# Interleaving the first two query chunks of a gated attention mix, with three more unused products at the start and 500 exponential tiles on VectorE

## The chip, the cores and the metric

The kernel runs on one core of one Trainium2 chip. The metric is the device time of one execution in microseconds (us). Engines are named as the profile names them: PE (TensorE, matrix products), ACT (ScalarE), DVE (VectorE), POOL (GpSimd), SP (SyncE, which here only issues transfers).

## The reference

The input x has 2048 tokens of 512 values, in bfloat16. Two branches share it, with 32 heads of 16 values each, and a gate mixes them:

```python
g = sigmoid((x * gate_w).sum(-1))
# branch A: softmax attention
q, k, v = split(x @ A_wqkv)
a = merge(softmax(q @ k.T * 16**-0.5) @ v) @ A_wo
# branch B: linear attention with learned features
pq, pk = q_B @ w_phi, k_B @ w_phi
phi = concat(softmax(p), softmax(-p))          # for pq and pk
b = merge((phi_q @ (phi_k.T @ v_B)) / (phi_q @ phi_k.sum(s) + 1e-6)) @ B_wo
out = g * a + (1 - g) * b
```

Branch A needs 32 x 2048 x 2048 exponentials; they are most of the work.

## The kernel before

**Tiles and passes.** The queries are cut into 4 chunks of 512 (`qc`), the keys into 16 tiles of 128 (`kt`). The 32 heads stand as 4 groups of 8 (`cp`, 128 rows of the projected q and k), and each group has two sides, so that 4 heads of one side lie in the four 32-row strips of PE. One pass `g` of 32 is a chunk, a group and a side; it has 16 rows `p` (one for each key tile) of 4 units (one for each head). A unit is a score tile of 128 keys x 512 queries. There are 512 rows and 2048 units. Before, the passes run through all four groups of chunk 0, then chunk 1, and so on.

**Two ways to an exponential.** Most units go to ACT: a PE product into one of four PSUM banks that form a ring (`_qk`, L1015), an exponential over two units at a time, 128x1024 (`_exp`, L1063), and one product with the values (`_pv`, L1122). `NUMS` gives for each pass how many of its 64 units go to DVE instead. These are taken in batches of four (`_vector_batch`): a score product into one of the other four PSUM banks, one DVE instruction that turns scores into bits of an exponential (128x512, L922), two DVE steps on the whole batch (128x2048 and 128x4096, L947), and four products with the values for each unit instead of one.

**Projections.** For each group, the keys of all 2048 tokens are projected before its first pass: 4 blocks, each with 4 products of 512 columns and one DVE copy out of PSUM (`_proj_k`, L698 and L770). Values are projected for two groups together: 8 blocks, each with 8 products of 256 columns, one DVE copy, and one POOL instruction for a scaled second copy (`_proj_v`, L809, L819, L826). Queries are projected for one chunk and group at a time (`_proj_q`): 4 products, one DVE copy (L783) and two POOL maskings (L788). `due` and `urgent` are counted in rows `p`: with one group after the other, group `cp` is first used in row 32 x `cp`.

**The rest.** The gate is computed once (`_gate`; its last part is four small DVE copies, L862). Branch B projects keys and queries in eight pairs of token tiles each, with a chain on DVE, POOL and ACT (L1281 to L1357), and its numerators are mixed into the outputs (`_out`, L1599). When a pass ends, DVE transposes its sums out of PSUM (L1143); every two passes are normalised on DVE and POOL (L1151 to L1160), and SP issues 16 small transfers and one transposing transfer into `onTA`.

**The order.** `Plan.order` places every operation in Python before the kernel runs: each engine gets a fixed queue, from the operations' modelled costs, `prio` (due row), `rel` and `urgent`. A pseudo-random shift of the due rows comes from `SEEDS`. Operations named in `PORT` on DVE are not placed beside a POOL operation. At run time each engine works through its queue in order and waits on semaphores. `filler` and `pad` put products with zeros (L1129), or unused products (L1035), into PE's queue where it would be little used; `PADK` is the number of the first ACT product that may be padded. `_warm` issues nine unused products at the start while the first part of x is loaded.

Of the kernel before, what the change touches and what calls it, by code (L numbers as in the profile page):

```python
# [10 lines left out]
P = 128  # L11
# [54 lines left out]
class Plan:  # L66
# [70 lines left out]
        self.ops.append(o)  # L137
        return o

    SEEDS = (6713, 8236, 795, 8928, 4203, 3987, 4548, 4431, 3369, 6855, 1992, 9096, 3816, 673, 8476, 4153, 2488, 5053, 9892, 380, 9864, 6961, 8928, 7398, 8610, 6258, 6732, 8778, 7190, 2318, 6568, 0, 527, 0)  # L140

    def shift(self):
        count = {}
# [30 lines left out]
    SAME = 100  # L174
    OPEN = 2
    HURRY, FREE = 20, 30
    PORT = ("v_step", "b_neg", "b_max", "b_sub", "b_sum", "b_total", "b_mul", "n_mul", "n_den", "kvbd")
    HOLDING = ("kproj", "qproj", "bv", "pq", "vproj", "outa", "outb", "wtr", "xtr")

    def rank(self, o):  # L180
# [227 lines left out]
class _Kernel:  # L408
# [13 lines left out]
    P_BACK, RATIO, BV = 1, 1, 8  # L422
    DEN, KV2, P_MAX = 1, 0, 0
    REND = 5
    P_M, P_BMUL, CHUNKS = 0, 0, 2
    GDUE = 26
    VMIN = 8
    FAST = 3
    VSOON = -2
    PADK = 8  # L430
    LAST, FIRST_OUT, NEXT_OUT, DEP_OUT = 0, 8, 0, 2
    ALONE, EARLY = 12, 10
    PVP = 10
# [1 line left out]
    def __init__(self, nc, A_x, A_wqkv, A_wo, B_wqkv, B_w_phi, B_wo, gate_w, out):  # L435
        self.nc = nc
        self.x2d = A_x.flatten_outer_dims()
        self.A_wqkv, self.A_wo = A_wqkv, A_wo
        self.B_wqkv, self.B_w_phi, self.B_wo = B_wqkv, B_w_phi, B_wo
        self.gate_w, self.out2d = gate_w, out.flatten_outer_dims()  # L440
        self.S = self.x2d.shape[0]
        self.NT = self.S // TOK
        self.NQC = self.S // QCH
        self.NPACK = self.NQC * 8 * self.NT
        self.plan = Plan()

    def build(self):
        with ExitStack() as ctx:
# [233 lines left out]
        job.bank = bank  # L682
        return job, (job if bank is None else None)

    def _warm(self, n, after):

        def run(e):
            for _ in range(n):
                ins = e.matmul(self.ps[:, 4, :], self.warm[:, 0:P], self.warm[:], start=True, stop=True)  # L689
            return ins  # L690
        self.plan.op("PE", run, 0.427 * n, reads=[self.b_warm], deps=[after], name="warm", prio=-99)

    COLS = 0

# [44 lines left out]
    def _proj_q0(self, half, bank):  # L739

        lo, op, ends = 256 * half, self.plan.op, []
        job, pool = self._job(bank)
        m = None
        for c in range(4):
            m = op("PE", lambda e, c=c: e.matmul(self._bank(job)[:, 0:256], self.WA[:, 0, c, 0:P],
                                                 self.xT[:, c, lo:lo + 256], start=(c == 0), stop=(c == 3)),
                   self.c_pe(256), reads=[self.b_x0[half], self.b_WA[0][0]], deps=[m], name="qproj", prio=half - 2.2,
                   acquire=None if c else pool)
            m.urgent = half - 99
        for side in range(2):  # L750
            dst, by = self.qT[:, side, lo:lo + 256], self.mask[:, side:side + 1]
            if half or side:
                o = op("DVE", lambda e, dst=dst, by=by: e.tensor_scalar(dst, self._bank(job)[:, 0:256], by, None,
                                                                        op0=ALU.mult), self.c_dve(256) + 0.06,
                       deps=[m] + ends, reads=[self.b_mask], name="q0_ev", prio=side - 2, release=pool if side else None)
            else:
                o = op("ACT", lambda e, dst=dst, by=by: e.activation(dst, self._bank(job)[:, 0:256], ACT.Copy, scale=by),
                       self.c_act(256) + 0.1, deps=[m], reads=[self.b_mask], name="q0_ev", prio=-2)
            self.b_qT[side].writers.append(o)
            if side == 0:  # L760
                self.b_q0[half].writers.append(o)
            ends.append(o)
        self.early.setdefault(bank, []).extend(ends)

    def _proj_k(self, cp, j):
        due = 32 * cp + 3 * j - self.KDUE if cp else 4 * j - 2.0
        self._proj(lambda c: self.WA[:, 1, c, P * cp:P * cp + P],
                   lambda c: self.xT[:, c, QCH * j:QCH * j + QCH],
                   [self.b_xT[j], self.b_WA[1][cp > 0]],
                   [lambda e, b: e.tensor_copy(self.kT[:, cp, QCH * j:QCH * j + QCH], b)],  # L770
                   self.c_dve(512), due, due - (24 if cp else 99), "kproj", [self.b_kT[cp][j]],
                   urgent=32 * cp + 4 * j - self.SOON)

    def _proj_q(self, qc, cp):
        n = qc * 4 + cp
        due = 32 * n - self.QDUE
        s0 = 2 * (n % (self.NQS // 2))

        lhs, rhs = lambda c: self.WA[:, 0, c, P * cp:P * cp + P], lambda c: self.xT[:, c, QCH * qc:QCH * qc + QCH]
        reads = [self.b_xT[qc], self.b_WA[0][cp > 0], self.b_mask]  # L780
        if self.P_Q:
            tmp, b_tmp = self.qtmp[:, n % 2, :], self.b_qtmp[n % 2]
            o = self._proj(lhs, rhs, reads, [lambda e, b: e.tensor_copy(tmp, b)], self.c_dve(512), due, 32 * n - 30, "qproj",  # L783
                           [b_tmp], urgent=32 * n - self.SOON)
            o.deps += [r for r in b_tmp.readers if r not in o.deps]
            b_tmp.readers = []
            for side in range(2):
                x = self.plan.op("POOL", lambda e, side=side: e.tensor_scalar(  # L788
                    self.qT[:, s0 + side, :], tmp, self.mask[:, side:side + 1], 0.0, op0=ALU.mult, op1=ALU.add), 0.7,
                    reads=[b_tmp, self.b_mask], writes=[self.b_qT[s0 + side]], name="qmask", prio=due + 1)  # L790
                x.urgent = o.urgent
            return
        self._proj(lhs, rhs, reads,
                   [lambda e, b: e.tensor_tensor(self.qT[:, s0:s0 + 2, :], b[:, None, :].to_broadcast([P, 2, QCH]),
                                                 self.mask[:, :, None].to_broadcast([P, 2, QCH]), ALU.mult)],
                   self.c_dve(1024), due, 32 * n - 30, "qproj", [self.b_qT[s0]], urgent=32 * n - self.SOON)
        self.b_qT[s0 + 1] = self.b_qT[s0]

    def _proj_v(self, pr, t0):

        op, NT = self.plan.op, self.NT
        job = Job()
        due = 64 * pr + t0 - (self.VDUE if pr else 0.5)
        mm = None
        for tt in range(2):
            def run(e, tt=tt):
                out = self._bank(job).rearrange("p (c t x) -> p c t x", c=2, t=2)[:, :, tt, :]
                for c in range(4):
# [2 lines left out]
                return ins  # L811
            mm = op("PE", run, 4 * self.c_pe(256), reads=[self.b_xT[t0 // 4], self.b_WA[2][pr]], deps=[mm], name="vproj",
                    prio=due, rel=due - 24 if pr else 0 if t0 < 4 else -99, acquire=None if tt else job)
            mm.urgent = 64 * pr + t0 - self.VSOON
        lo, n = t0 * self.VCP, 2 * self.VCP
        both = lambda v: v[:, 2 * pr * NT * self.VCP:(2 * pr + 2) * NT * self.VCP].rearrange(
            "p (c x) -> p c x", c=2)[:, :, lo:lo + n]
# [47 lines left out]
                prio=100))  # L865
        self.b_gB.writers = done

    NUMS = (6, 10, 12, 14, 14, 15, 13, 16, 13, 20, 17, 13, 16, 13, 19, 21, 10, 18, 12, 16, 19, 13, 17, 16, 15, 20, 12, 19, 17, 16, 23, 13)

    def _plan_vector(self):  # L870

# [9 lines left out]
            self.hooks.setdefault(max(0, int(due) - 4), []).append(  # L881
                lambda k=k, units=units, due=due: self._vector_batch(k, units, due))
        for n in range(1, 4 * self.NQC):
            self.hooks.setdefault(max(0, 32 * n - 30), []).insert(0, lambda n=n: self._proj_q(*divmod(n, 4)))
        self.away = set(away)

    def _value_bufs(self, bufs, p, spill):

        kt, cp = p % self.NT, p // (2 * self.NT) % 4
        at = cp * self.NT + kt  # L890
        found = list(bufs[cp][kt // 2].writers)
        if spill and at + 1 < 4 * self.NT:
            found += bufs[(at + 1) // self.NT][(at + 1) % self.NT // 2].writers
        return found

    def _vector_batch(self, number, units, due):
# [46 lines left out]
        for k in range(4):  # L943
# [9 lines left out]
            for g in sorted({u // (4 * NT) for u in units}):  # L953
# [3 lines left out]

                def run(e, g=g, src=src, ot=ot, v=v, tile=tile, place=place):
                    for j, u in src:
                        ins = self._values(e, ot, g % 8, u // 4 % NT, {u % 4: tile[:, place(j), :].bitcast(BF16)}, v)  # L960
                    return ins
                x = op("PE", run, 0.23, reads=[buf], deps=list(found.values()), name="pvx", prio=units[0] / 4 - 2,
                       kind="col", array=0.0533 * len(src), strips=[u % 4 for _, u in src])
# [5 lines left out]
    def _attention(self):  # L969
# [24 lines left out]
        while a < len(self.mine):  # L994
# [4 lines left out]
            done = self.mine[a] if a < len(self.mine) else NU  # L999
            while len(self.pvs) < done // 4:  # L1000
                self._pv(len(self.pvs))
                if len(self.pvs) % (8 * NT) == 0:
                    self._out(len(self.pvs) // (8 * NT) - 1)

    def _unit(self, u):

        p, i = divmod(u, 4)
        g, kt = divmod(p, self.NT)
        qc, g8 = divmod(g, 8)
        s = 2 * ((qc * 4 + g8 // 2) % (self.NQS // 2)) + g8 % 2  # L1010
        return p, i, kt, g8 // 2, s

    def _scores(self, e, u, out, cols=slice(0, QCH)):
# [56 lines left out]
    def _pv(self, p):  # L1070
# [13 lines left out]
        def run(e):  # L1084
            for _ in range(o.filled):
                self._fill(e, ot)
            return self._values(e, ot, g % 8, kt, src, self.V)
        o = self.plan.op("PE", run, 0.23, reads=[self.b_zero], deps=deps, name=f"pv{p}", prio=p + self.PVP, kind="col",
                         acquire=None if kt else ot, array=0.0533 * len(src), strips=list(src))
        plan = self.plan  # L1090
# [40 lines left out]
        return ins  # L1131

    def _norm_a(self, g, last):
        qc, g8 = divmod(g, 8)
        return self._norm(qc, lambda: self._bank(self.ot[g]), g8 % 2, last, self.onTA[:, qc % 3, g8 // 2, :],
                          self.b_onTA[qc % 3][g8 // 2], 16 * g + 17.0, self.ot[g], g >= self.NPACK // self.NT - 2)

# [430 lines left out]
    def _out(self, qc):  # L1568
        op, NT, NQC = self.plan.op, self.NT, self.NQC
        for tt in range(4):  # L1570
            t = 4 * qc + tt
            final = qc == NQC - 1
            due = max(128 * (qc + 1) + 8 + 4 * tt, self._num_due(t) + 8)
            job, first = self.outs[t]
            b_onTA = self.b_onTA[qc % 3]
            if final:
# [70 lines left out]
```

## Time and profile before

| | value |
|---|---|
| time, median of 3 runs | 767.77 us (766.18 to 769.58) |
| profiled execution: its time | 767.62 us |
| profiled execution: span, first to last instruction | 765.6 us |
| ACT busy | 749.1 us, 804 instructions |
| DVE busy | 711.6 us, 1110 instructions |
| PE busy | 739.6 us, 7149 products |
| POOL busy | 207.5 us |
| mean granted PE clock | 0.997 |
| ACT exponentials (L1063) | 782 instructions, 720.4 us |
| DVE tiles (L922) and their steps (L947) | 488 and 244 instructions, 313.7 and 235.4 us |
| first exponential starts, last one starts | 8.22 us, 756.5 us |

Busy time is the union of an engine's or a group's instruction spans. Consecutive instructions of an engine overlap by some tens of ns, so a mean duration times a count is more than the busy time. A PE product's span holds the time to pass through the array, and products overlap; PE's busy share says little of how full it is.

### The profile page before, as it was taken

The numbers are of one execution on the slowest core, as the hardware profiler recorded it, in microseconds if no ns is written. First come the engines' busy times: TensorE is split into PE (matmuls) and PEld (weight loads), VectorE is DVE, ScalarE is ACT, GpSimd is POOL, SyncE is SP. The second block draws the span as 40 slices with busy tenths as digits, with TensorE's granted clock in tenths as the row PEclk, the third lists the DMA queues.
The fourth block names the chain that finished last, engine by engine and source line by source line (L and its number), as shares of the span: only waits on it lengthen the run. The fifth ranks groups of instructions, "written<-read, shape, count | busy, mean of one in ns | idle before, by whom it ended". The sixth has DMA issues, their size and how long they took to land.

```text
span 765.6 us, 17042 instructions
## 1 busy us (share of the span) xinstructions
PE 739.6 (97%) x7149; PEld 219.6 (29%) x7220; DVE 711.6 (93%) x1110; ACT 749.1 (98%) x804; POOL 207.5 (27%) x301
## 2 busy tenths in 40 slices
PE   8999999999999999999999999999999999999998
PEld 3322233222222222222332322232222222222222
DVE  4778997899999999999999999999999999999995
ACT  6999999999999999999999999999999999999996
POOL 2210255315053260405145023422314140250000
PEclk9999999999999999999999999999999999999999
DMA  9501001000000000010121202211111121011000
GB/s 232 127 2 28 3 14 15 1 2 8 9 3 14 1 3 14 1 15 2 15 29 28 53 11 51 45 27 30 32 26 28 29 47 24 15 30 27 5 12 28
DMA packets 89180, 20.78 MB, mean 27 GB/s; under 512 B 83472, under 2 KB 88592, under 8 KB 89104
## 3 DMA queue, kind: packets, MB, share of 16 engines
q1 hardware_dynamic: 87232, 18.92, 13.4%
q8 instruction: 56, 0.92, 0.5%
q10 hardware_dynamic: 1872, 0.79, 0.4%
q14 instruction: 20, 0.16, 0.1%
HBM read 4.21 MB, written 2.10 MB: 8 GB/s over the span
## 4 chain that ended last, share of the span: by engine, by line
ACT 76%; PE 15%; DVE 9%; issue 1%
ACT ET L1063 73%; PE ps L1015 5%; PE ps L1122 5%; PE ps L698 3%; ACT bq L1310 3%; DVE vs L922 3%; DVE vs L947 2%; PE ps L1129 1%; PE ps L689 1%; DVE onB L1475 1%; DVE T L1143 0%; DVE bq L1307 0%; DVE btree L1304 0%; DVE ghB L862 0%; DVE qtmp L783 0%
## 5 line engine op out<-in xcount | busy, mean ns | idle before, releaser
L1063 ACT ACTIVATE ET<-ps 128x1024 bf16<-128x1024 f32 (+1 forms) x782 | 720.4, 1154 | 3.7 <-PE ps L1015 3.6
L922 DVE TENSOR_SCALAR vs<-ps 128x512 uint16<-128x512 f32 x488 | 313.7, 679 | 20.7 <-PE ps L1015 19.7
L1015 PE MATMUL ps<-qT,kT 32*128 32x512 bf16 (+1 forms) x2052 | 312.4, 385 | 13.1 <-ACT ET L1063 8.0
L947 DVE TENSOR_SCALAR vs<-vs 128x2048 uint16<-128x2048 uint16 (+1 forms) x244 | 235.4, 977 | 1.9 <-PE ps L1122 0.5
L1122 PE MATMUL ps<-vs,V 128*32 128x512 bf16 x1952 | 216.4, 384 | 1.4 <-DVE vs L947 1.4
L1122 PE MATMUL ps<-ET,V 128*32 128x512 bf16 x1560 | 194.5, 387 | 0.1
L1015 PEld LDWEIGHTS ps<-qT,kT 32*128 32x128 bf16 x2052 | 78.0, 91 | 309.3 <-ACT ET L1063 293.2
L1314 POOL TENSOR_TENSOR btree<-btree 128x512 f16<-128x512 f16 (+1 forms) x32 | 33.4, 1044 | 188.8 <-DVE btree L1312 188.0
L1122 PEld LDWEIGHTS ps<-ET,V 128*32 128x32 bf16 x1560 | 48.9, 94 | 84.1 <-issue 75.8
L1129 PE MATMUL ps<-kT,zero 128*32 128x512 bf16 x628 | 63.4, 385 | 0.0
L1122 PEld LDWEIGHTS ps<-vs,V 128*32 128x32 bf16 x1952 | 49.8, 95 | 45.9 <-issue 27.5
L1299 POOL TENSOR_SCALAR bq<-bq 128x1024 bf16<-128x1024 bf16 x16 | 21.5, 1341 | 150.6 <-DVE bq L1281 119.5
L698 PE MATMUL ps<-WB,xT 128*128 128x512 bf16 x160 | 49.6, 383 | 2.8 <-issue 2.1
L1160 POOL TENSOR_TENSOR T<-T,rinv 128x512 bf16<-128x512 f32 x15 | 18.2, 1210 | 83.4 <-DVE rinv L1158 83.2
L698 PE MATMUL ps<-xT,WA 128*128 128x512 bf16 x101 | 33.2, 392 | 1.9 <-issue 1.6
L788 POOL TENSOR_SCALAR qT<-qtmp,mask 128x512 bf16<-128x512 bf16 x30 | 25.8, 866 | 28.8 <-DVE qtmp L783 28.5
L1143 DVE STREAM_TRANSPOSE T<-ps 128x512 f32<-128x512 f32 x32 | 22.6, 707 | 11.2 <-PE ps L1122 11.1
L1310 ACT ACTIVATE bq<-bq 128x2048 bf16<-128x2048 bf16 x16 | 32.1, 2007 | 0.2
L1281 DVE CAST bq<-ps 128x512 bf16<-128x512 f32 x32 | 21.7, 680 | 0.3 <-PE ps L698 0.2
L826 POOL TENSOR_SCALAR V<-V 128x544 bf16<-128x544 bf16 x16 | 12.6, 788 | 33.4 <-DVE V L819 33.2
L698 PEld LDWEIGHTS ps<-WB,xT 128*128 128x128 bf16 x192 | 13.3, 97 | 25.3 <-issue 20.5
L1129 PEld LDWEIGHTS ps<-kT,zero 128*32 128x32 bf16 x628 | 14.7, 94 | 19.7 <-issue 18.8
(88 smaller groups left out, 405.3 us busy)
## 6 DMA issues: line engine op xcount, KB each, us to landing
T<-T SPq DMA_DIRECT2D x240, 8.0 KB, 1.8
WB<-in_B_wqkv_dram SPq DMA_DIRECT2D x1, 1536.0 KB, 7.9
out_dram<-WB SPq DMA_DIRECT2D x12, 128.0 KB, 1.7
WA<-in_A_wqkv_dram SPq DMA_DIRECT2D x2, 384.0 KB, 5.4
WoB<-in_B_wo_dram SPq DMA_DIRECT2D x1, 512.0 KB, 3.8
WoA<-in_A_wo_dram SPq DMA_DIRECT2D x1, 512.0 KB, 4.8
WA<-in_A_wqkv_dram ACTq DMA_DIRECT2D x2, 128.0 KB, 3.1
WA<-in_A_wqkv_dram ACTq DMA_DIRECT2D x1, 256.0 KB, 4.6
```

What stands on the lines that cost most here:

```text
L698: return e.matmul(out, lhs, rhs, start=start, stop=stop)
L788: x = self.plan.op("POOL", lambda e, side=side: e.tensor_scalar(self.qT[:, s0 + side, :], tmp, self.mask[:, side:side + 1], 0.0, op0=ALU.m ...
L922: bits = lambda e, to, src: e.tensor_scalar(to, src, SCALE * LOG2E * 128.0, float(ORIGIN), op0=ALU.mult, op1=ALU.add)
L947: o = op("DVE", lambda e, k=k, src=src, dst=dst: e.tensor_scalar(dst, src, float(STEPS[k - 1]), None, op0=ALU.add), 0.16 + k * n * QCH * 0 ...
L1015: return e.matmul(out[:, cols], self.kT[32 * i:32 * i + 32, cp, kt * TOK:(kt + 1) * TOK], self.qT[32 * i:32 * i + 32, s, cols], start=True ...
L1063: o = plan.op("ACT", lambda e: e.activation(self.ET[:, a % NS:a % NS + n, cols], self.ps[:, a % NR:a % NR + n, cols], ACT.Exp, scale=SCALE ...
L1122: ins = e.matmul(self._bank(ot)[32 * i:32 * i + 32, :], v[:, v0:v0 + 32], tile, start=(kt == 0), stop=(kt == self.NT - 1), tile_position=( ...
L1129: ins = e.matmul(self._bank(ot)[32 * i:32 * i + 32, :], self.zero[:], self.kT[:, 0, 0:QCH], start=False, stop=False, tile_position=(0, 32 ...
L1143: t1 = op("DVE", lambda e: e.transpose(T1[:, side].rearrange("p b s -> p (b s)"), src()), 0.735, deps=last, writes=[b_T1[side]], name="n_t ...
L1281: [lambda e, b, k=k: e.tensor_copy(bq[:, k].rearrange("p (g s v) -> p g s v", g=8, s=2)[:, :, 0, :], b.rearrange("p (g v) -> p g v", g=8))],
L1310: op("ACT", lambda e: e.activation(flat, flat, ACT.Exp), 1.789, reads=[b], writes=[b], name="b_exp", prio=due + 1)
L1314: + [("b_sum", two(128 * n), lambda e, n=n: e.tensor_tensor(half[:, :, 0:n], half[:, :, 0:n], half[:, :, n:2 * n], ALU.add), (n <= self.P_ ...
```

## The change

Chunks 0 and 1 are interleaved: the passes now go through group 0 of chunk 0, group 0 of chunk 1, group 1 of chunk 0, group 1 of chunk 1, and so on; chunks 2 and 3 stay as they were. Group `cp` is then first used in row 64 x `cp`, and the due rows of its key and value projections follow. The first value block of the second half keeps an earlier due row, because a read of 32 columns runs on into it. `_warm` is used a second time: three unused products behind the first half of the first query projection. `PADK` goes from 8 to 2, the gate's copies and `gwb` join `PORT`, `NUMS` gives 500 units to DVE instead of 488 (+11 in passes 0 to 7, -5 in 8 to 15, +6 in 16 to 23, none in 24 to 31), and `SEEDS` is another list.

```diff
-    PORT = (..., "n_mul", "n_den", "kvbd")
+    PORT = (..., "n_mul", "n_den", "kvbd", "gate_b", "gwb")
...
+    PAIRQ = 1
...
-    PADK = 8
+    PADK = 2
...
+        pairs = [(qc, cp) for cp in range(4) for qc in range(2)] if self.PAIRQ else [(qc, cp) for qc in range(2) for cp in range(4)]
+        self.pairs = pairs + [(qc, cp) for qc in range(2, self.NQC) for cp in range(4)]
+        self.seq = [(qc, 2 * cp + side) for qc, cp in self.pairs for side in range(2)]
+        self.use = [32 * next(n for n, x in enumerate(self.pairs) if x[1] == cp) for cp in range(4)]
+        self.done = [32 * max(n + 1 for n, x in enumerate(self.pairs) if x[0] == qc) for qc in range(self.NQC)]
...
+        if self.WARM and not half:
+            self.early.setdefault(1, []).append(self._warm(self.WARM, m, bank=1, cost=0.215, prio=-2.15))
...
-        due = 32 * cp + 3 * j - self.KDUE if cp else 4 * j - 2.0
+        due = self.use[cp] + 3 * j - self.KDUE if cp else 4 * j - 2.0
...
-                   urgent=32 * cp + 4 * j - self.SOON)
+                   urgent=self.use[cp] + 4 * j - self.SOON)
...
-        due = 64 * pr + t0 - (self.VDUE if pr else 0.5)
+        use = self.use[2 * pr] + t0
+        if pr and not t0:
+            use = min(use, self.use[1] + 31)
+        due = use - (self.VDUE if pr else 0.5)
...
-    NUMS = (6, 10, 12, 14, 14, 15, 13, 16, 13, 20, 17, 13, 16, 13, 19, 21, 10, 18, 12, 16, 19, 13, 17, 16, 15, 20, 12, 19, 17, 16, 23, 13)
+    NUMS = (6, 10, 16, 14, 14, 16, 16, 19, 13, 19, 17, 12, 17, 11, 19, 19, 14, 20, 12, 16, 19, 13, 17, 16, 15, 20, 12, 20, 17, 16, 22, 13)
...
-                if len(self.pvs) % (8 * NT) == 0:
-                    self._out(len(self.pvs) // (8 * NT) - 1)
+                if len(self.pvs) in self.done:
+                    self._out(self.done.index(len(self.pvs)))
...
-            due = max(128 * (qc + 1) + 8 + 4 * tt, self._num_due(t) + 8)
+            due = max(self.done[qc] + 8 + 4 * tt, self._num_due(t) + 8)
```

More of the change, by code (lines that the diff above doesn't have):

```diff
@@ L138, in op @@
         return o
-    SEEDS = (6713, 8236, 795, 8928, 4203, 3987, 4548, 4431, 3369, 6855, 1992, 9096, 3816, 673, 8476, 4153, 2488, 5053, 9892, 380, 9864, 6961, 8928, 7398, 8610, 6258, 6732, 8778, 7190, 2318, 6568, 0, 527, 0)
+    SEEDS = (3340, 2114, 9789, 849, 7476, 9797, 2928, 4117, 3297, 4434, 5571, 2308, 3491, 3547, 0, 2037, 1043, 5479, 6702, 2263, 0, 95, 4494, 8165, 7230, 4451, 7158, 3400, 9901, 9455, 1584, 0, 4360, 0)
     def shift(self):
@@ L176 @@
     HURRY, FREE = 20, 30
-    PORT = ("v_step", "b_neg", "b_max", "b_sub", "b_sum", "b_total", "b_mul", "n_mul", "n_den", "kvbd")
+    PORT = ("v_step", "b_neg", "b_max", "b_sub", "b_sum", "b_total", "b_mul", "n_mul", "n_den", "kvbd", "gate_b", "gwb")
     HOLDING = ("kproj", "qproj", "bv", "pq", "vproj", "outa", "outb", "wtr", "xtr")
@@ L683, in _job, with _warm @@
         return job, (job if bank is None else None)
-    def _warm(self, n, after):
+    def _warm(self, n, after, bank=4, cost=0.427, prio=-99):
         def run(e):
             for _ in range(n):
-                ins = e.matmul(self.ps[:, 4, :], self.warm[:, 0:P], self.warm[:], start=True, stop=True)
+                ins = e.matmul(self.ps[:, bank, :], self.warm[:, 0:P], self.warm[:], start=True, stop=True)
             return ins
-        self.plan.op("PE", run, 0.427 * n, reads=[self.b_warm], deps=[after], name="warm", prio=-99)
+        return self.plan.op("PE", run, cost * n, reads=[self.b_warm], deps=[after], name="warm", prio=prio)
+    WARM = 3
     COLS = 0
@@ L771, in _proj_k, with _proj_q @@
                    self.c_dve(512), due, due - (24 if cp else 99), "kproj", [self.b_kT[cp][j]],
-                   urgent=32 * cp + 4 * j - self.SOON)
-    def _proj_q(self, qc, cp):
-        n = qc * 4 + cp
+                   urgent=self.use[cp] + 4 * j - self.SOON)
+    def _proj_q(self, n):
+        qc, cp = self.pairs[n]
         due = 32 * n - self.QDUE
@@ L813, in _proj_v @@
                     prio=due, rel=due - 24 if pr else 0 if t0 < 4 else -99, acquire=None if tt else job)
-            mm.urgent = 64 * pr + t0 - self.VSOON
+            mm.urgent = use - self.VSOON
         lo, n = t0 * self.VCP, 2 * self.VCP
@@ L883, in _plan_vector @@
         for n in range(1, 4 * self.NQC):
-            self.hooks.setdefault(max(0, 32 * n - 30), []).insert(0, lambda n=n: self._proj_q(*divmod(n, 4)))
+            self.hooks.setdefault(max(0, 32 * n - 30), []).insert(0, lambda n=n: self._proj_q(n))
         self.away = set(away)
     def _value_bufs(self, bufs, p, spill):
-        kt, cp = p % self.NT, p // (2 * self.NT) % 4
+        kt, cp = p % self.NT, self.pairs[p // (2 * self.NT)][1]
         at = cp * self.NT + kt
@@ L959, in run @@
                     for j, u in src:
-                        ins = self._values(e, ot, g % 8, u // 4 % NT, {u % 4: tile[:, place(j), :].bitcast(BF16)}, v)
+                        ins = self._values(e, ot, self.seq[g][1], u // 4 % NT, {u % 4: tile[:, place(j), :].bitcast(BF16)}, v)
                     return ins
@@ L1008, in _unit @@
         g, kt = divmod(p, self.NT)
-        qc, g8 = divmod(g, 8)
-        s = 2 * ((qc * 4 + g8 // 2) % (self.NQS // 2)) + g8 % 2
+        g8 = self.seq[g][1]
+        s = 2 * (g // 2 % (self.NQS // 2)) + g8 % 2
         return p, i, kt, g8 // 2, s
@@ L1086, in run @@
                 self._fill(e, ot)
-            return self._values(e, ot, g % 8, kt, src, self.V)
+            return self._values(e, ot, self.seq[g][1], kt, src, self.V)
         o = self.plan.op("PE", run, 0.23, reads=[self.b_zero], deps=deps, name=f"pv{p}", prio=p + self.PVP, kind="col",
@@ L1133, in _norm_a @@
     def _norm_a(self, g, last):
-        qc, g8 = divmod(g, 8)
+        qc, g8 = self.seq[g]
         return self._norm(qc, lambda: self._bank(self.ot[g]), g8 % 2, last, self.onTA[:, qc % 3, g8 // 2, :],
```

## The prediction

> **What bounds the kernel now.** I read the page's first two parts, the chain, ACT's and DVE's idle time, then windows. The page, engines and 40 slices:
>
> ```profile
> PE 739.6 (97%) x7149; PEld 219.6 (29%) x7220; DVE 711.6 (93%) x1110; ACT 749.1 (98%) x804; POOL 207.5 (27%) x301
> PE   8999999999999999999999999999999999999998
> ...
> DVE  4778997899999999999999999999999999999995
> ACT  6999999999999999999999999999999999999996
> ```
>
> ACT is full from the second slice to the last but one; DVE has gaps in the first eight slices only. PE's 9 says little, since product spans overlap. The chain that ended last, in order of time:
>
> ```profile
> 14.54 72.58 ACT ET L1063 x79
> ...
> 393.13 2.50 DVE vs L922 x4
> 395.63 0.60 DVE vs L947
> ...
> 396.82 1.14 DVE vs L947
> ```
>
> The chain is ACT's exponentials (73% of the span), one each 72.58/79 = 0.92 us; between 393 and 509 us it runs through DVE and PE. So DVE is nearly co-bound there, at 0.60 to 0.63 us a tile and 0.60 + 1.14 us a batch for the steps. The waits of ACT, and windows by stage:
>
> ```profile
> ACT ET L1063 <- PE ps L1015: 3.6, 6, 1.4
> ```
>
> ```profile
> 0.00:24.00 24.00, 21.75 (x120) 8.20 (x121) 13.12 (x24) 16.64 (x21) 6.26 (x18) 0.93 1.08 235
> 24.00:168.00 144.00, 140.25 (x1214) 43.81 (x1227) 122.35 (x187) 142.61 (x155) 37.04 (x51) 1.00 0.08 17
> 168.00:744.00 576.00, 559.63 (x5672) 162.01 (x5721) 563.08 (x880) 575.05 (x614) 164.17 (x232) 1.00 0.12 21
> 744.00:765.60 21.60, 17.98 (x151) 5.59 (x151) 13.09 (x23) 14.80 (x17) 0.00 (x0) 0.98 0.08 25
> ```
>
> Columns after the length: PE, PEld, DVE, ACT, POOL busy, then PE's clock. ACT loses 3.6 us inside its exponentials in all. DVE's idle time is 10.9, 21.7, 12.9 and 8.5 us: 54.0 together. The first part (x lands) and the last (last values, norm, output) are the same in both programs; the 34.6 us between are what the change can spend.
>
> **ACT's gain.** 12 units leave ACT: 6 exponentials of two units, 782 to 776. At 0.92 us: 5.5 us, all on ACT's path.
>
> **DVE's cost.** 12 tiles at 313.7/488 = 0.643 us, and three batches' steps at 235.4/122 = 1.93 us: 7.7 + 5.8 = 13.5 us. The rows' busy times sum to 765 us where DVE was busy 711.6, as spans overlap, so this is 13.5 x 0.93 = 12.6 us: DVE 724.2 us. With first and last part as before, and 2.0 us from span to time, time = 724.2 + 10.9 + 8.5 + 2.0 + M = 745.6 + M, where M is DVE's idle time in the middle. (Before: 711.6 + 21.4 + 34.6 = 767.6.) For ACT's gain to arrive M must fall to about 16.
>
> **What the interleaving moves.** In the built order, set beside ACT's exponentials, the key blocks of group 1 go from 40-59 us to 83-109, those of group 2 from 86-105 to 142-177, those of group 3 from 148-171 to 233-286, and the second half's values from 99-136 to 130-225. Some ten blocks leave the first 192 us: about 10 x 0.64 us of DVE copies (6.5 us, filled by the 11 new tiles of passes 0 to 7), 4 x 4 products of 0.22 us and six times 8 of 0.11 us on PE (some 8.5 us). That matters since PE is what kept DVE waiting there: the zero products (L1129), which fill PE's spare time, are 8 in the first 168 us, and 620 later. The moved value blocks take their POOL copies (0.79 us each) along; POOL is at 27%. They issue no transfers. In SP's queue the 16 mixing transfers and one transpose per two passes keep their number; near row 225 two transposes of branch B go ahead of one of these. Chunk 0's outputs stay bound by branch B's numerators (row 233). All this at nothing: PE's and POOL's later slack hides it; without that cover the PE part costs its 8.5 us.
>
> **Is there room?** I counted, for each DVE tile, the DVE work queued ahead of it, and ACT's work ahead of its score product in PE's order, with the durations above. The difference is DVE idle time that the order leaves at least. Before: 32.7 us at pass 6 (measured by 168 us: 32.5) and 43.5 at the end, which with the 2.1 us that ACT lost in the middle is the 45.5 measured by 744 us. After: 20.8 at pass 5, then flat, even 20.1 at passes 21 and 22, and 23.0 at the end. So the order asks DVE to run 550 us with no gap at all, beside an ACT with none. Neither can make good what the other loses.
>
> **New stalls.** Before, the same count is flat (37.0 to 37.5) from pass 17 to 25, some 190 us, and ACT lost 0.55 + 0.17 us there. Flat over 550 us: 0.72 x 550/190 = 2.1 us; and 0.7 us where the count falls: 2.8. Lower bound 0 (it can hide nowhere else, but need not occur); upper bound 18, if M stays at 34.6. I take 2.8, by the nearest stretch. The old 0.72 is taken out against it.
>
> **The gate's copies.** ACT's longest stall, 1.39 us, is here (timeline):
>
> ```profile
> 89.92 2.01 DVE L862 COPY ghB<-gh 32x16 f32<-32x16 f32 x4
> 89.97 1.06 POOL L1160 TENSOR_TENSOR T<-T,rinv 128x512 bf16<-128x512 f32 x1 [0.62 <-DVE rinv L1158]
> ...
> 92.70 0.38 PE L1015 MATMUL ps<-qT,kT 32*128 32x512 bf16 x1 [1.28 <-DVE kT L770]
> ...
> 94.20 2.94 ACT L1063 ACTIVATE ET<-ps 128x1024 bf16<-128x1024 f32 x3 [1.39 <-PE ps L1015]
> ```
>
> Four copies in a row, two slowed beside POOL, hold up a key copy, PE's queue behind it, and ACT. Afterwards the copies stand apart between tiles, and keys are due twice as late. Between 0 and 1.4 us; I take 1.4.
>
> **The start.** The windows there, same columns:
>
> ```profile
> 8.00:9.00 1.00, 0.65 (x7) 0.26 (x5) 0.96 (x3) 0.78 (x2) 0.00 (x0) 1.00 0.86 178
> 9.00:10.00 1.00, 0.70 (x7) 0.22 (x7) 0.39 (x2) 1.00 (x3) 0.00 (x0) 1.00 1.13 215
> 10.00:12.00 2.00, 2.00 (x9) 0.44 (x9) 0.93 (x3) 1.45 (x3) 0.00 (x0) 0.61 1.11 214
> 12.00:14.00 2.00, 2.00 (x8) 0.69 (x7) 1.11 (x2) 1.94 (x2) 0.00 (x0) 0.54 1.08 251
> ```
>
> PE was 65 to 70% busy for 2 us, and then its granted clock was halved for 4 us; ACT stalled 0.55 and 0.50 us just there. The three products and two padding ones fill those gaps: gain at most 1.05 us. They cost at most 3 x 0.43 us (nine took 4.02) less the 0.38 us that PE waits for x anyway, 0.9 us, since the first score product now stands behind them. I take a gain of 0.4. The Trainium skill ("TensorE: Matmul & The Clock Gate", Part 1) has the clock fall only after an idle window of about 3.4 us; here it fell with PE busy 0.65 and 0.70, so the measurement decides. By the page the filling would gain nothing, and the sum would be 0.4 us more.
>
> **The sum.** 767.62 - 5.5 (exponentials) - 1.4 (gate) - 0.7 (old stalls) - 0.4 (start) + 2.8 (new stalls) = 762.4 us. The profiled run lies 0.15 us from the median of 767.77, so I make no correction. It needs M = 16.8. About 0.5%, 3.8 us, is what a measurement of this kernel can tell: below 763.9 is faster, above 771.6 slower.
>
> **Rivals.**
>
> 1. DVE eats the gain (0.18, no change): new stalls not 2.8 but 5 to 9 us, 764.6 to 768.6. For it: the flat count, and DVE waits for score products (19.7 us in 50 waits) that a fixed order can't move. Against: with more queued it waits less, and a PE with fewer projections answers sooner.
> 2. Slower (0.06): the early waits stay, because it was not PE that caused them. M then keeps its 21.7 us from 24 to 168 us and at least 6 of the later 12.9: 745.6 + 27.7 = 773.3 us; with all 34.6, 780. It decides from M = 26 on. Against: the few zero products early.
> 3. POOL holds DVE (0.05, no change). The steps have a mean of 1.24 us where the chain has 1.14, and the longest of them took 1.95; gate copies took 0.48. With no DVE slack each such meeting goes to the end; four like the gate's cost 5.6 us: 768.0. Against: 6 more steps are 2% more chances, and the order keeps such pairs apart. The Trainium skill ("SBUF — State Buffer", Who interferes with whom) says that such a DVE instruction and POOL lock each other out for a whole instruction, which speaks against this change; the trace agrees in the 2.01 us of the gate's copies.
> 4. The change doesn't do what it says (0.02, no change): exponentials start later by as much as they are fewer, for instance by a later gate: 767.
>
> **How the numbers follow.** The forecast has the rest, 0.69, all of it faster: 759.0 (no new stalls, all 1.05 at the start) to 763.9. With 0.25 for no change (rivals 1, 3, 4) and 0.06 slower. The range goes from 759.0 to 767.0: it takes in the forecast and over half of rival 1, and leaves out about 2 in 10. The likeliest, 762.4, is the time.
>
> **What would show it.** Right: 776 exponentials, ACT busy 743 to 744 us, DVE 723 to 726; DVE idle from 24 to 168 us down from 21.7 to about 11; ACT's waits for score products 3 to 5 us, in many small pieces after 100 us; the clock above 0.9 from 10 to 14 us; no 1.39 us stall at the gate. Wrong: M over 18.3, with the chain on DVE for most of the span (rival 1 or 2), or steps whose mean rises above 1.3 us for 128x4096 (rival 3).

## The result and the profile after

The changed kernel takes 758.84 us (median of 4 runs, 758.10 to 759.25) where the kernel before takes 768.43 us on the same chip: a ratio of 0.9881, with a 95% interval from 0.9857 to 0.9905. It is 9.6 us faster, 3.6 us below the forecast of 762.4 and 0.2 us below 759.0, the lower end of the range. Beside the last four experiments one execution of the kernel before, out of 20, took 1508 us, and the intervals leave it out. The profiled execution took 758.10 us with a span of 756.1 us; line numbers are 13 higher than before in most places (L1063 is now L1076, L922 is L935).

The page of the changed kernel, engines and slices:

```profile
PE 745.0 (99%) x7234; PEld 220.1 (29%) x7234; DVE 717.3 (95%) x1128; ACT 742.4 (98%) x798; POOL 210.2 (28%) x301
...
DVE  5788999999999999999999999999999999999994
ACT  6999999999999999999999999999999999999996
```

DVE is now full from the fifth slice on instead of the ninth. Its busy time has grown by 5.7 us only, ACT's has fallen by 6.7. The groups of exponentials, tiles and steps (count | busy, mean ns | idle before):

```profile
L1076 ACT ACTIVATE ET<-ps 128x1024 bf16<-128x1024 f32 (+1 forms) x776 | 714.6, 1155 | 1.7 <-PE ps L1028 1.5
L935 DVE TENSOR_SCALAR vs<-ps 128x512 uint16<-128x512 f32 x500 | 322.6, 684 | 10.7 <-PE ps L1028 8.9
...
L960 DVE TENSOR_SCALAR vs<-vs 128x2048 uint16<-128x2048 uint16 (+1 forms) x250 | 240.3, 972 | 1.3 <-PE ps L1135 0.5
```

776 exponentials, 5.8 us less than before. The tiles' waits for score products fell from 19.7 to 8.9 us. All waits of ACT, and the windows that answer to the four of before (the last is again 21.6 us long; columns as before):

```profile
ACT xT L1609 <- PE ps L706: 3.6, 1, 3.6
ACT qT L765 <- DVE kT L743: 3.0, 1, 3.0
ACT L663 <- issue: 2.3, 1, 2.3
ACT ET L1076 <- PE ps L1028: 1.5, 3, 0.7
```

```profile
0.00:24.00 24.00, 21.81 (x134) 8.59 (x134) 13.52 (x25) 17.14 (x22) 6.25 (x18) 1.00 1.04 225
24.00:168.00 144.00, 143.34 (x1284) 43.34 (x1281) 132.43 (x210) 143.90 (x157) 37.42 (x59) 1.00 0.09 19
168.00:734.50 566.50, 561.31 (x5684) 162.64 (x5678) 560.22 (x876) 566.38 (x607) 166.55 (x224) 1.00 0.12 21
734.50:756.10 21.60, 18.57 (x148) 5.53 (x141) 11.11 (x20) 15.01 (x18) 0.00 (x0) 1.00 0.08 25
```

ACT's three waits for score products end at 12.0 us at the latest. From 24 to 734.5 us it is idle 0.2 us in 710.5: the stall at the gate's copies and both later ones are gone. DVE's idle time is 10.5, 11.6, 6.3 and 10.5 us; the second was 21.7. The chain that ended last has long pieces of exponentials again, and stretches that run through PE or DVE, the main ones from 73 to 103 us, 326 to 397 us and 663 us to the end:

```profile
12.01 53.26 ACT ET L1076 x58
...
353.18 4.27 DVE vs L935 x7
...
397.46 39.51 ACT ET L1076 x43
```

DVE still takes 4.27/7 = 0.61 us a tile where it runs without a gap.

### The profile page after: what moved, and what is told of

Same layout as the page of the kernel before. It is cut to its first block, busy times and chain, and to the rows that moved or that the text cites. A ratio compares the mean times of both kernels' runs of the same rounds, so it can differ in the third digit from the quotient of the medians.

```text
span 756.1 us, 17157 instructions
## 1 busy us (share of the span) xinstructions
PE 745.0 (99%) x7234; PEld 220.1 (29%) x7234; DVE 717.3 (95%) x1128; ACT 742.4 (98%) x798; POOL 210.2 (28%) x301
## 3 DMA queue, kind: packets, MB, share of 16 engines
q1 hardware_dynamic: 87232, 18.92, 13.2%
## 4 chain that ended last, share of the span: by engine, by line
ACT 74%; PE 17%; DVE 7%; DMA 1%; issue 0%
ACT ET L1076 71%; PE ps L1135 7%; PE ps L1028 6%; ACT bq L1323 3%; DVE vs L935 3%; PE ps L706 3%; DVE vs L960 2%; PE ps L1142 1%; DMA xT<-in_A_x_dram 1%; DVE onB L1488 0%; DVE bq L1320 0%; DVE btree L1317 0%; DVE T L1156 0%; DVE btree L1315 0%; PE ps L714 0%
## 5 line engine op out<-in xcount | busy, mean ns | idle before, releaser
L1076 ACT ACTIVATE ET<-ps 128x1024 bf16<-128x1024 f32 (+1 forms) x776 | 714.6, 1155 | 1.7 <-PE ps L1028 1.5
L935 DVE TENSOR_SCALAR vs<-ps 128x512 uint16<-128x512 f32 x500 | 322.6, 684 | 10.7 <-PE ps L1028 8.9
L1028 PE MATMUL ps<-qT,kT 32*128 32x512 bf16 (+1 forms) x2052 | 307.3, 384 | 4.7 <-ACT ET L1076 2.3
L960 DVE TENSOR_SCALAR vs<-vs 128x2048 uint16<-128x2048 uint16 (+1 forms) x250 | 240.3, 972 | 1.3 <-PE ps L1135 0.5
L1135 PE MATMUL ps<-vs,V 128*32 128x512 bf16 x2000 | 211.8, 384 | 0.9 <-DVE vs L960 0.7
L1327 POOL TENSOR_TENSOR btree<-btree 128x512 f16<-128x512 f16 (+1 forms) x32 | 38.5, 1202 | 212.7 <-DVE btree L1325 211.5
L706 PE MATMUL ps<-WB,xT 128*128 128x512 bf16 x192 | 58.6, 384 | 0.1
L798 POOL TENSOR_SCALAR qT<-qtmp,mask 128x512 bf16<-128x512 bf16 x30 | 29.9, 1001 | 33.0 <-DVE qtmp L793 32.8
L706 PE MATMUL ps<-xT,WA 128*128 128x512 bf16 x120 | 38.1, 384 | 0.1
L706 PE MATMUL ps<-WoA,onTA 128*128 128x512 bf16 x64 | 19.8, 383 | 0.0
```

The costliest lines, as they stand in the source:

```text
L706: return e.matmul(out, lhs, rhs, start=start, stop=stop)
L935: bits = lambda e, to, src: e.tensor_scalar(to, src, SCALE * LOG2E * 128.0, float(ORIGIN), op0=ALU.mult, op1=ALU.add)
L960: o = op("DVE", lambda e, k=k, src=src, dst=dst: e.tensor_scalar(dst, src, float(STEPS[k - 1]), None, op0=ALU.add), 0.16 + k * n * QCH * 0 ...
L1028: return e.matmul(out[:, cols], self.kT[32 * i:32 * i + 32, cp, kt * TOK:(kt + 1) * TOK], self.qT[32 * i:32 * i + 32, s, cols], start=True ...
L1076: o = plan.op("ACT", lambda e: e.activation(self.ET[:, a % NS:a % NS + n, cols], self.ps[:, a % NR:a % NR + n, cols], ACT.Exp, scale=SCALE ...
L1135: ins = e.matmul(self._bank(ot)[32 * i:32 * i + 32, :], v[:, v0:v0 + 32], tile, start=(kt == 0), stop=(kt == self.NT - 1), tile_position=( ...
```

## Experiments

Two of the theories were open after the first result: which of the small gains at the gate and the start the program owns, and whether DVE is really without spare time.

**The changed kernel again**, as a base for the next three on the same chip.

> The changed kernel once more, beside the next three on the same chip, as their base. Expected 758 to 760 us, and ACT without a stall over 0.3 us between 20 and 740 us. Its start should show whether the full clock that PE already had for the first key products (4 products in 0.62 us, where the kernel before took 1.04 us) is the program's doing or differs from one execution to the next: the nine products ahead of them are the same in both programs.

758.95 us (758.54 to 758.99). One stall in the middle, 0.16 us at 519 us. Its first four key products took 1.04 us, as in the kernel before, where the first profile of the same program showed 0.62. So PE's speed at the very start differs from one execution to the next, and with it the fourth whole exponential started at 14.2 us here (13.8 us in the first profile, 14.5 before). The Trainium skill ("TensorE: Matmul & The Clock Gate", Part 1) calls the number of slow products at a start run-variable, because the window that watches PE runs freely; these starts agree in that they vary, but do not show the window.

**The gate's copies in a row.**

```diff
-    PORT = (..., "n_den", "kvbd", "gate_b", "gwb")
+    PORT = (..., "n_den", "kvbd")
```

> The gate's copies are taken out of PORT again. In the built order only DVE's queue differs: the four gate copies stand in a row, as before, where the changed kernel has tiles, steps and copies between them; every other engine's order is the same. Theory (the row of copies caused the 1.39 us stall, and with the lost overlap some 1.6 us): 1.0 to 1.6 us more than the changed kernel, with a stall of ACT near the copies. Rival (the keys due twice as late took the stall away, since nothing urgent stands behind the copies any more): within 0.3 us of the changed kernel and no such stall.

759.86 us (759.38 to 760.43), 0.9 us above the base, just under what the theory expected, and the runs' ranges don't touch. The timeline:

```profile
80.53 1.79 DVE L875 COPY ghB<-gh 32x16 f32<-32x16 f32 x4
80.84 1.05 POOL L1173 TENSOR_TENSOR T<-T,rinv 128x512 bf16<-128x512 f32 x1
...
84.36 2.85 ACT L1076 ACTIVATE ET<-ps 128x1024 bf16<-128x1024 f32 x3 [0.23 <-PE ps L1028]
...
87.66 1.02 ACT L1076 ACTIVATE ET<-ps 128x1024 bf16<-128x1024 f32 x1 [0.45 <-PE ps L1028]
```

In a row the four copies last 1.79 us, two of them 0.37 and 1.0 us; apart they take 0.16 to 0.17 us each. The two slow ones began while a POOL instruction ran and ended 0.02 and 0.03 us after it. ACT loses 0.68 us in two stalls soon after, and 0.69 us at 520 us instead of the base's 0.16. So it is the placement beside POOL that costs, and PORT is what took it away; a row of copies away from POOL was not run. The Trainium skill ("SBUF — State Buffer", Who interferes with whom) has a POOL instruction and a DVE instruction that uses both port pairs, as a copy can, lock each other out: the second waits for the whole of the first. A copy of 0.17 us that becomes 1.0 us next to a POOL instruction of 1.05 us agrees.

**The unused products at the start.** In the first run the three products are left out, in the second the padding too:

```diff
-    WARM = 3
+    WARM = 0
...
-    PADK = 2
+    PADK = 8
```

> The three unused products at the start are left out; the two padding products ahead of the fifth score product stay. Only PE's first 15 rows differ. Theory (they keep the clock up): PE's granted clock falls to about half somewhere between 10 and 14 us, ACT gets two stalls of about 0.5 us there, and the time is 0.5 to 1.0 us more. Rival (the clock depends on when the execution began, not on these products, or the padding suffices): clock 1.0 there and the time within 0.3 us, or less by up to 0.4 us, as the score product no longer stands behind them.

> The three unused products and the early padding are both left out, so that PE starts as in the kernel before. Theory: the start is 0.7 us slower, as the two traces show it (14.54 us against 13.84 us for the fourth whole exponential), with the clock at 0.5 to 0.6 from 10 to 14 us. Rival (the difference of the starts was the execution's, not the program's): within 0.3 us of the changed kernel.

758.20 us (758.11 to 758.72) without the products, and 758.36 us (757.46 to 760.62) without either: both medians are below the base's 758.95. Both theories failed, and both medians lie some 0.3 us lower than even the rivals allowed. The windows of the second, same columns:

```profile
10.00:12.00 2.00, 1.83 (x8) 0.46 (x8) 1.12 (x2) 1.62 (x3) 0.00 (x0) 0.64 1.10 217
12.00:14.00 2.00, 2.00 (x9) 0.60 (x7) 0.78 (x2) 1.65 (x2) 0.00 (x0) 0.51 1.13 261
```

Without the padding PE's clock fell to 0.64 and 0.51 as it did before, and still the median didn't rise: ACT's stalls at the start were 0.47, 0.68 and 0.38 us, against 0.65, 0.53 and 0.32 us in the base. The median hides that the clock did not fall every time. In the second run the three executions with a mean clock of 1.0 took 757.46 to 758.36 us, the two with 0.998 and 0.996 took 759.14 (the profiled one) and 760.62 us. The run e10 below starts like the kernel before, with neither products nor padding, and its profiled execution kept the clock (two windows, then ACT's timeline):

```profile
10.00:12.00 2.00, 1.91 (x12) 0.55 (x11) 1.39 (x3) 1.90 (x3) 0.00 (x0) 1.00 1.06 220
12.00:14.00 2.00, 2.00 (x16) 0.96 (x15) 1.15 (x3) 2.00 (x3) 0.00 (x0) 1.00 1.09 245
```

```profile
8.15 8.87 ACT L1063 ACTIVATE ET<-ps 128x512 bf16<-128x512 f32 x11 [1.19 <-PE ps L1015]
```

Its first eleven exponentials run without a stall, and the fourth whole one starts at 13.2 us, as in e12. Where the clock fell it starts at 14.5 (before) and 14.8 us (e4), with products and padding at 13.7 to 14.2 us (first profile, e1, e2, e9, e11). So these unused products cost 0.4 to 1.1 us where the clock holds without them, and save 0.3 to 1.1 us where it would have fallen; on the medians here that comes to nothing. The first run has the lowest median of all, 0.75 us or 0.1% below its base, though its slowest execution lies above the base's fastest.

**Parts alone.** Four kernels each undo or do one part: the tiles (NUMS of before in the changed kernel; NUMS of after in the one before), the seeds (all zero), and seeds and interleaving together.

```diff
 e5:  changed kernel   -    NUMS = (6, 10, 16, 14, ...)   +    NUMS = (6, 10, 12, 14, ...)
 e6:  kernel before    -    NUMS = (6, 10, 12, 14, ...)   +    NUMS = (6, 10, 16, 14, ...)
 e7:  changed kernel   -    SEEDS = (3340, ...)           +    SEEDS = (0,) * 34
 e8:  as e7            -    PAIRQ = 1                     +    PAIRQ = 0
```

> The changed kernel with the kernel before's NUMS: 488 tiles on DVE, chunks interleaved, same seeds (tuned for the other NUMS). Leaves 12 units more on ACT. Theory (the number of tiles is the gain of 5.5 us; the interleaving is what makes room for them): 6 more exponentials at 0.92 us on a path of ACT without stalls, 758.9 + 5.5 = 764.5 us, within 1 us; the count of DVE work in the built order leaves 49.6 us idle, so no stall is due. Rival (the interleaving itself shortens the path, by fewer stalls, and the tiles add little): 761 or less.

> The kernel before with the changed kernel's NUMS alone: 500 tiles, no interleaving, seeds of the kernel before. Theory (no room without the interleaving): the count of DVE work falls from 39.6 us at pass 17 to 25.4 at pass 25 below its own earlier level, so DVE is asked for 14 us more than ACT's time there and ACT stalls by 5 to 14 us: 766 to 775 us, with DVE idle from 24 to 168 us still over 18 us and stalls of ACT from 400 to 600 us. Rival (DVE takes 12 tiles anywhere, as its rows get cheaper without gaps): 767.9 - 5.5 = 762.4 us or less.

> The changed kernel with all SEEDS zero: the due rows are not shifted at random. Theory (the interleaving makes the room, the seeds only smooth the order): the count of DVE work rises to 38.1 us and falls by 3 to 6 us twice, so 3 to 8 us of stalls: 762 to 767 us. Rival (the gain is the seeds' doing): 768 or more, no better than the kernel before.

> As the run without seeds, and without the interleaving: 500 tiles, chunks one after the other. Beside that run it shows what the interleaving is worth when no order was searched for either. Theory (PE has no spare time before 170 us without it, so DVE waits there and pays later): 3 to 8 us above the run without seeds, DVE idle from 24 to 168 us over 18 us against under 15. Rival (the interleaving gives nothing by itself): within 2 us of that run.

| kernel | median us | ratio to before, 95% interval |
|---|---|---|
| e5, interleaved, 488 tiles, seeds of after | 782.28 | 1.0187, 1.0170 to 1.0203 |
| e6, not interleaved, 500 tiles, seeds of before | 802.07 | 1.0460, 1.0425 to 1.0494 |
| e7, interleaved, 500 tiles, no seeds | 788.73 | 1.0269, 1.0249 to 1.0289 |
| e8, not interleaved, 500 tiles, no seeds | 794.37 | 1.0353, 1.0320 to 1.0386 |

All four are far slower than either kernel. e5 and e6 missed both of their expectations, by 18 and 27 us; e7 came out as its rival had it, and e8 as expected beside e7. Waits of ACT in e5, then of e7:

```profile
ACT xT L1609 <- PE ps L706: 10.5, 2, 10.0
ACT ET L1076 <- PE ps L1135: 7.5, 1, 7.5
```

```profile
ACT ET L1076 <- PE ps L1135: 17.6, 8, 5.7
ACT xT L1609 <- PE ps L706: 11.5, 1, 11.5
```

The loss is in few long stalls. One of e7's, from the timeline:

```profile
517.68 0.62 PE L1135 MATMUL ps<-vs,V 128*32 128x512 bf16 x8
518.23 0.56 PE L1453 MATMUL ps<-kvbd,phiT 128*128 128x4 bf16 x16
...
523.28 0.40 PE L1135 MATMUL ps<-ET,V 128*32 128x512 bf16 x4
...
523.74 2.85 ACT L1076 ACTIVATE ET<-ps 128x1024 bf16<-128x1024 f32 x3 [5.73 <-PE ps L1135]
```

ACT waits for a product with the values to read an exponential (ET) and so free its slot; PE works on DVE's tiles and on branch B in the meantime and comes to the ET products of the pass only at 523.28 us. It is a matter of the order alone, and my count of DVE work doesn't see it: for e5 it left 49.6 us idle and no stall. The end is late too: ACT waits 10 to 11.6 us for its last output copy where the changed kernel waits 3.6. So NUMS, SEEDS and the order of passes hold only together: without its seeds the changed kernel has no gain at all, and none of e5 to e7 prices a part. What can be read is where DVE has gaps, from the windows of e5 and e6:

```profile
24.00:168.00 144.00, 142.09 (x1244) 42.39 (x1242) 123.41 (x196) 143.74 (x156) 37.86 (x59) 1.00 0.09 18
24.00:168.00 144.00, 143.12 (x1247) 44.95 (x1245) 122.38 (x189) 137.91 (x150) 36.00 (x51) 1.00 0.08 17
```

DVE is idle for 20.6 us there with the interleaving alone and for 21.6 us with the tiles alone, against 21.7 us before and 11.6 us with both, which fits the reading that the one makes room and the other fills it. At the same 500 tiles and without seeds it is 13.9 us with the interleaving (e7) and 18.7 us without (e8). Their times differ by 5.6 us, as expected (3 to 8). But ACT waits 23.4 us for products in e7 and 26.8 us for products and DVE in e8, most of it after 400 us, and from 24 to 168 us it loses nothing in e7 and 1.3 us in e8. One pair of such orders doesn't show that the 5.6 us are the interleaving's.

**More work, same order.** Since a part can't be taken away alone, I added work without moving anything: some tiles computed twice on DVE, or some exponentials twice on ACT, the first time into a spare tile.

```diff
-   lambda e, j=j, job=job: bits(e, va[:, 0, j, :], self._bank(job))
+   lambda e, j=j, job=job: [bits(e, x, self._bank(job)) for x in
+       ([self.spare[:, 0:QCH].bitcast(U16)] if (4 * number + j) % 30 == 15 else []) + [va[:, 0, j, :]]][-1]
...
-   lambda e: e.activation(self.ET[...], self.ps[...], ACT.Exp, scale=SCALE)
+   lambda e: [e.activation(y, self.ps[...], ACT.Exp, scale=SCALE) for y in
+       ([self.spare[:]] if k % 120 == 60 else []) + [self.ET[...]]][-1]
```

> The changed kernel with 17 of its 500 tiles computed twice on DVE, the first time into a spare tile, spread evenly; every engine's order stays as it is, and nothing else is added. DVE gets 17 x 0.61 = 10.4 us more. Theory (after the change DVE has no spare time, its order leaves it no gap for 550 us): 6 to 10 us more than the changed kernel's 758.9 us, 765 to 769 us, in stalls of ACT. Rival (ACT bounds it and DVE's idle time of 39 us takes the work): under 3 us more, 759 to 762 us.

> The same in the kernel before: 16 of its 488 tiles computed twice, 9.8 us more on DVE, order unchanged. Theory (before the change DVE had spare time, 54 us idle in all, but little of it where the chain runs through DVE from 393 to 509 us, a fifth of the additions): 2 to 5 us more than 767.9 us, clearly less than the changed kernel loses. Rival (DVE is as tight in both): within 1.5 us of the changed kernel's loss.

> The changed kernel with 6 of its two-unit exponentials computed twice on ACT, the first time into a spare tile, spread from the 60th to the 660th; order unchanged. It puts back on ACT what the 12 tiles took off, without moving anything. Theory (ACT's work is the path from end to end): 6 x 0.92 = 5.5 us more than 758.9 us, 764.4 us, within 0.7. Rival (DVE is the path, and ACT has slack beside it): under 3 us more.

> The same in the kernel before: 6 exponentials twice, order unchanged. Theory (ACT is the path there too, with short stretches on DVE that were never late): 5 to 5.5 us more than 767.9 us, 773.2 us, within 0.7. Rival (the stalls and the stretch on DVE and PE from 393 to 509 us are a bound of their own, and part of the added work falls into waits): 2 to 4 us more.

| added | median us | ratio to before, 95% interval | more than its base |
|---|---|---|---|
| DVE, 17 tiles, after | 765.45 | 0.9973, 0.9962 to 0.9985 | 6.5 us |
| DVE, 16 tiles, before | 771.80 | 1.0067, 1.0042 to 1.0091 | 4.2 us |
| ACT, 6 exponentials, after | 764.61 | 0.9956, 0.9936 to 0.9977 | 5.7 us |
| ACT, 7 exponentials, before | 773.65 | 1.0089, 1.0066 to 1.0113 | 6.0 us |

(Bases: 758.95 and 767.63 us. The first is e1's, from another chip, on which the kernel before took 767.89 us. In the kernel before, 7 exponentials were doubled instead of the 6 expected, since it has 782.) Work on ACT comes out in full in both: 0.94 us per exponential after, 0.86 before, where the chain says 0.92. Work on DVE comes out too, 0.38 us a tile after and 0.26 before, of 0.61. e9, e11 and e12 came out as their theories had it. e10 lies in its range, but whether the kernel before pays less for DVE's work, as its theory had it, stays open: its interval is 3.2 to 7.0 us. ACT's waits with the added tiles, and the groups of tiles:

```profile
ACT ET L1076 <- PE ps L1028: 4.5, 13, 0.7
```

```profile
L935 DVE TENSOR_SCALAR vs<-ps 128x512 uint16<-128x512 f32 x500 | 321.6, 679 | 8.7 <-PE ps L1028 7.6
...
L935 DVE TENSOR_SCALAR spare<-ps 128x512 uint16<-128x512 f32 x17 | 11.6, 682 | 0.7 <-PE ps L1028 0.6
```

13 waits in place of 3, none over 0.7 us: the added work is felt in small stalls all along. They are 2.8 of the 6.5 us (4.5 against 1.7 in e1). Another 3.1 us stand in ACT's busy time, 745.8 us against 742.7 in e1 for the same work: by the traces an exponential overlaps the one ahead by 0.19 us in the median where it was 0.26. Both engines are on the path in both kernels, ACT in full and DVE by about half.

## Why the direction was right, and where the terms were off

**Exponentials, -5.5 us.** Right: their busy time fell by 5.8 us, and e11 gives 5.7 for the same work put back in the same order.

**The gate, -1.4, and the old stalls, -0.7.** All three stalls are gone. They were worth more than their idle time: an exponential lasts 1.16 us and the next starts 0.92 us after it, so each gap also costs that overlap, 0.24 us. Three gaps make 2.11 + 0.72 = 2.8 us, not 2.1. For the gate, e2 shows that about 0.9 us come from placing the copies: it keeps the later due rows and still has 0.68 us of stalls behind them. What the due rows gave beyond that is open.

**New stalls, +2.8.** This is the term that failed, and the only large one. There are none: 0.2 us of ACT's idle time from 24 to 734.5 us. The step behind it was DVE's cost, of which I forecast 12.6 us more busy time; it grew by 5.7 us, from 711.6 to 717.3 (716.9 in e1). The added work itself was priced well: 12 tiles at 0.61 us from start to start and three batches' steps at 0.60 + 1.14 us are 12.5 us. What I left out is that the rest of DVE's work gets shorter. The gate's copies fell from 1.9 to 0.7 us. And instructions that follow one another without a gap overlap by some 0.08 us, so that each gap that closes also takes 0.08 us off the busy time: by the traces 942 instructions overlapped the next before and 1004 after, 44 more beside the 18 added ones, which is worth 3.5 us (waits of DVE went from 74 to 48). The steps' mean fell from 977 to 972 ns, worth 1.2 us. That makes 5.9 of the 6.8 us between 12.5 and 5.7; the rest is open. The Trainium skill ("Perfetto Trace Analysis", Optimizing Scalar/DVE Operations) says that an instruction's overhead for reaching its data lasts about twice as long in the profile as it keeps the engine busy, since its second half runs beside the next instruction; a tile of 0.68 us that takes 0.61 us in a run agrees. So the "550 us with no gap" that the count asked of DVE had some 7 us of slack, and M came out at 17.9 us beside a forecast of 16.8 with DVE's work 7 us smaller. That this slack is why the stalls stayed away is supported by e9: with 17 more tiles DVE was busy for 725.8 us, close to the 724.2 forecast, and there ACT's waits for score products did grow, by the 2.8 us that the forecast had for new stalls (such a close agreement is luck). They came with 6.5 us more time, so the price of 2.8 us was too low as well, for want of the lost overlap.

**What the interleaving moves.** Right in its sign and place: DVE's idle time from 24 to 168 us fell from 21.7 to 11.6 us, with "about 11" forecast; e5 and e6 show that neither the order nor the tiles do this alone. Whether 500 tiles could have been had without the interleaving, in an order searched for them, no run shows.

**The start, -0.4.** The clock did stay at 1.0 from 10 to 14 us, but the reading behind the term was wrong. I took the fall of the clock for what this start does. It is what the profiled execution did: e10 and e12 have the same start, the same 1.35 us of PE's work from 8 to 10 us, and no fall. Of 35 executions of the kernel before beside the experiments, the 13 with a mean clock of 0.999 or more took 766.1 to 766.7 us, 11 with 0.997 or 0.998 took 767.6 to 768.0, and 10 with 0.995 or 0.996 took 769.0 to 769.5 (one with 0.989: 773.5). All eight of the changed kernel (the result and e1) had 1.0. At a clock of 0.999 or more the two kernels are 7.4 us apart by their medians, 766.3 and 759.0; about 2 of the 9.6 us go with executions of the kernel before in which the clock fell. Where it fell is known only for the profiled ones.

**The sum.** 5.5 (exponentials) + 2.8 (three stalls with their overlap) + 0.7 (start, in this profile) + 0.2 (from the last exponential to the end, 7.9 and 7.7 us) = 9.2 of the 9.5 us between the two profiled executions. At equal clock the start turns into a loss of 0.6 to 1.0 us (13.8 and 14.2 against 13.2), and 5.5 + 2.8 + 0.2 less that is 7.5 to 7.9 us, beside the 7.4 measured. Without the term for new stalls the forecast would have been 759.6. Two signs of being right failed with that term: DVE was to be busy 723 to 726 us and was for 717.3, and ACT was to wait 3 to 5 us for score products, in small pieces after 100 us, and waited 1.5 us, all of it by 12 us. ACT's busy time, 742.4 us, lies just under its 743 to 744.

**The rivals.** Rival 1 needed ACT stalls of 5 us and more; there were none, though e9 shows how near they are: 10.4 us more on DVE take back 6.5 of the 8.9 us between e1 and the kernel before beside it. Rival 2 fell with the early idle time. Rival 3 is real as a mechanism (e2), but the order keeps such pairs apart. Rival 4 fell with the exponentials.

## What to carry to other kernels

When work is added to a nearly full engine, count not only the new work, by the distance between starts, but also what the old work saves as its gaps close; and price a stall of a pipelined engine by its idle time plus the overlap that its last instruction loses. In a kernel whose order is searched for, a part that is undone alone shows the loss of the search and not the worth of the part: add or repeat work in a fixed order instead, or repeat a comparison over several orders before a difference is put down to the part. Read the clock of every execution before the start of one profile is taken for the program's. Keep small copies of one engine away from long instructions of another that shares its port; four of them cost 0.9 us here.

## What the runs showed of the hardware

PE's clock was at 0.50 for 3.4 us (from 10.4 us on before, from 10.6 us on in e4), with PE busy 1.35 and 1.46 of the 2.00 us from 8 to 10. The busy share alone doesn't decide it: in e3, e10 and e12 it was 1.35 of 2.00 too, and the clock stayed at 1.0. With the three products and the padding it stayed at 1.0 there in all five profiles (first profile, e1, e2, e9, e11), with the padding alone in one (e3). What decides is open. Such a fall put the fourth whole exponential 1.3 to 1.6 us later, and the profiled execution of the kernel before took 1.3 us more than its median at a clock of 0.999 or more. Whether the first key products run fast differs between executions of the same program (0.62 and 1.04 us for four).
